# Attention with V and 64 columns of ones as weights: outputs that leave PE transposed, sums repeated 64-fold, normalisation by Exp of minus Ln

## The chip, the cores and the metric

The kernel runs on one core of one Trainium2 chip. The metric is the device time of one execution in microseconds (us); lower is better. Engines are called as the profile calls them: PE (TensorE, matmul), PEld (its weight loads, which overlap PE: 53% and 96% of the span in the kernel before), DVE (VectorE), ACT (ScalarE), POOL (GpSimd), SP (SyncE).

## The reference, cut to what matters

```python
# q, k, v: 8 batches, 8 heads, 576 tokens, 64 per head
scores = 1 / sqrt(64) * q @ k.T
mask_local   = (rel >= 0) & (rel < 32)                       # heads 0 to 3
mask_strided = (rel >= 0) & (pos % 32 equal for both tokens) # heads 4 to 7
attn = exp(scores - max); attn /= attn.sum()
x = (attn @ v) as 4608 tokens x 512
out = ((x @ w1) * (x @ w2)) @ w3 @ w_out                     # 512 -> 1024 -> 1024 -> 512
```

The masks leave little work: each query block of a local head meets one key block of 128, each group of four residue classes (72 queries) of a strided head one block of 96 keys. The products of the last two weights (w3 @ w_out) are folded into one 1024x512 weight at the start of the kernel. The large part is the feed-forward product, nine tiles of 512 tokens.

## The kernel before

Work is written as operations with an engine, an assumed duration, dependences and the buffers they take and give. A greedy scheduler inside the kernel turns them into one fixed order per engine. Each engine then runs its order, with semaphores between them. So an operation that is longer than the scheduler thought delays all that stands behind it on its engine: in the changed kernel, below, one PV starts 2.84 us after its masks are done, because other groups stand before it on PE.

The kernel divides PSUM into four single banks ("f": feed-forward groups, transposes, folding) and two double banks ("B": scores S and PV results X). A "pair" below is two heads of one batch; there are 32, 16 local and 16 strided. Each pair is computed in two halves, g = 0 and 1. The parts that the change touches, with cuts marked:

```python
plan = Plan(dict(f=NF, B=2, stg=NSTG, pte=3, asb=2, osb=3, xqs=4, w3n=4, abt=4))   # buffers of each kind
v16L = [consts.tile([P, 4, LT, D + 1], FP16, ...) for i in range(2)]    # V and one column of ones
# ...
for g in range(2):                                                      # two halves of a pair
    # S: scores, transposed (keys on partitions); one B slot
    pin(nc.tensor.matmul(sps[:, h, i * w:(i + 1) * w], kT[r_, ks:ks + P], qT[r_, hp, qs:qs + w], ...))
    # exp on ACT: PSUM -> SBUF, float16; the B slot is free again
    pin(nc.scalar.activation(out=pte[0:kr], in_=bank("B", sk)[0:kr, :, 0:288], func=AF.Exp, ...))
    # mask on DVE, float16 -> float16
    pin(nc.vector.tensor_mul(ptm..., pte..., mask...))
    # PV: the probabilities are the weights, [V|1] streams: 65 columns; queries on partitions
    pin(nc.tensor.matmul(xps[:, h, i * 65:(i + 1) * 65], ptms[pslot][0:kr, c0:c0 + P],
                         vt[0:kr, 2 * (hp % 2) + h, g * m + i, :], start=True, stop=True))
    # norm on DVE: one reciprocal per query and head, one product
    pin(nc.vector.reciprocal(out=rcp[0:w, :, 0:m], in_=xv[:, :, :, D]))
    pin(nc.vector.tensor_mul(xqs..., xv[:, :, :, 0:D], rcp...))
# U: transposes of the normalised outputs on PE, then a copy (DVE or ACT) into xT, the feed-forward input
pin(nc.tensor.transpose(ps[:, t * w:(t + 1) * w], live[("xqs", ...)]..., id16[0:w, 0:w]))
# ... feed-forward per tile of 512 tokens: 8 x (a: 4 matmuls, copy asb on ACT; b: 4 matmuls, product on DVE),
# then 4 x (o: 8 matmuls, copy osb on ACT, store issued from ACT)
```

The softmax here doesn't subtract the row's maximum and nothing guards it: scores larger than these inputs give would overflow.

## Time and profile before

| before | value | view |
|---|---|---|
| time | 283.07 us median of 2 (282.9 to 283.25) | runs |
| PE busy | 270.5 us, 96% of the span | the page, part 1 |
| ACT busy, DVE busy | 155.4 us (55%), 166.3 us (59%) | the page, part 1 |
| PE's share of the chain of waits | 83% | the page, part 4 |
| granted PE clock | full in every slice | the page, part 2 |

From the page of the kernel before: busy time per engine (us, share of the span, instructions), the granted clock in 40 slices (tenths), and the first line of the chain that ended last.

```profile
PE 270.5 (96%) x2540; PEld 150.5 (53%) x2540; DVE 166.3 (59%) x326; ACT 155.4 (55%) x291; POOL 123.2 (44%) x146
...
PEclk9999999999999999999999999999999999999999
...
PE 83%; DMA 8%; DVE 4%; SPq 1%; ACT 1%; POOL 1%; issue 0%; ACTq 0%; POOLq 0%; DVEq 0%
```

From the groups of instructions, each shape apart (line, engine, operation, out<-in, count | busy us, mean ns of one | idle before it and who ended that idle time).

```profile
L669 DVE TENSOR_TENSOR ptm<-pte,maskS 96x576 f16<-96x576 f16 x32 | 22.0, 726 | 0.2 <-ACT pte L661 0.2
L697 DVE TENSOR_TENSOR xqs<-ps_X,rcp 72x512 f16<-72x512 f32 x32 | 22.0, 687 | 1.1
L661 ACT ACTIVATE pte<-ps_S 96x576 f16<-96x576 f32 x32 | 19.1, 643 | 5.7 <-PE ps_S L650 5.7
L696 DVE RECIPROCAL rcp<-ps_X 72x8 f32<-72x8 f32 x32 | 6.4, 201 | 10.8 <-PE ps_X L682 10.5
L696 DVE RECIPROCAL rcp<-ps_X 96x6 f32<-96x6 f32 x32 | 5.9, 186 | 6.9 <-PE ps_X L682 6.5
L330 ACT ACT_TABLE_LOAD x1 | 1.3, 1283 | 0.8 <-PEq L825 0.8
```

PE is nearly always busy, and ACT and DVE wait for it. The activation tables are loaded once, in 1.28 us. What the output transposes really cost is read from the timeline, by the distance of one group's start to the next (start us, duration us, engine, line, operation); the durations themselves overlap (the first group below, 129.08 + 0.35 us, ends after the second has started at 129.26 us).

```profile
129.08 0.35 PE L682 MATMUL ps_X<-v16L,ptm 128*128 128x65 f16 x6
129.26 0.61 PE L614 MATMUL ps_T<-id,x 128*128 128x128 f16 x8
...
131.90 0.43 PE L708 MATMUL ps_U<-id,xqs 96*128 96x96 f16 x6
132.16 1.03 PE L740 MATMUL ps_a<-xT,w1h 128*128 128x512 f16 x4
```

A half of PV takes 0.18 us of PE here, and the six output transposes 0.26 us (those of a strided pair 0.27 us).

### The profile page before, as it was taken

Reading aid. Unit: us, or ns where it says so; the run is one execution under the profiler, and the core shown is the slowest. Engines: PE = TensorE matmul, PEld = TensorE weight load, DVE = VectorE, ACT = ScalarE, POOL = GpSimd, SP = SyncE. Lnnn points to the kernel's source line nnn. Section 1 sums busy time; section 2 is a strip of 40 time slices with the busy share of each in tenths; the row PEclk is TensorE's granted clock in tenths of the full one; section 3 lists DMA queues with packets and bytes.
Section 4 is the critical chain, followed back from the end, with each engine's and each line's share of the span. In section 5 each row is a group of like instructions: output and inputs, shape, how many; then the busy total and the mean of one; then the engine's idle time right before and its main releaser. Section 6 shows DMA issues by size and latency. Waiting matters only on the chain.

```text
span 282.0 us, 6430 instructions
## 1 busy us (share of the span) xinstructions
PE 270.5 (96%) x2540; PEld 150.5 (53%) x2540; DVE 166.3 (59%) x326; ACT 155.4 (55%) x291; POOL 123.2 (44%) x146
## 2 busy tenths in 40 slices
PE   4989989999999999999799999999999999999995
PEld 1468876456555555555455555555555554444443
DVE  4037486876668788856885668466746673320320
ACT  2386576448665665666357656765666543324322
POOL 5876898699669685772956352100000000000000
PEclk9999999999999999999999999999999999999999
DMA  6999999996779678978973800210021003003003
GB/s 222 323 376 358 279 357 355 240 294 235 246 185 356 170 241 243 278 248 233 337 159 102 302 2 2 94 58 0 3 112 40 0 4 147 2 0 149 0 3 149
DMA packets 53679, 48.66 MB, mean 173 GB/s; under 512 B 21008, under 2 KB 45840, under 8 KB 53648
## 3 DMA queue, kind: packets, MB, share of 16 engines
q1 hardware_dynamic: 48320, 38.81, 46.2%
q10 hardware_dynamic: 5328, 9.44, 8.9%
q8 instruction: 20, 0.33, 0.5%
q14 instruction: 11, 0.09, 0.1%
HBM read 38.80 MB, written 9.44 MB: 171 GB/s over the span
## 4 chain that ended last, share of the span: by engine, by line
PE 83%; DMA 8%; DVE 4%; SPq 1%; ACT 1%; POOL 1%; issue 0%; ACTq 0%; POOLq 0%; DVEq 0%
PE ps_a L740 22%; PE ps_b L757 21%; PE ps_o L777 21%; PE ps_X L682 5%; PE ps_T L614 4%; DMA st<-in_moe_w_dram 4%; PE ps_S L650 4%; PE ps_U L708 3%; DMA st<-in_moe_w_out_dram 3%; DVE ptm L669 3%; PE ps_mm L543 3%; DMA st<-in_k_dram 2%; SPq L293 1%; DVE xT L288 1%; DVE abt L763 0%; ACT qT L286 0%
## 5 line engine op out<-in xcount | busy, mean ns | idle before, releaser
L763 DVE TENSOR_TENSOR abt<-ps_b,asb 128x512 f16<-128x512 f32 x72 | 49.5, 688 | 53.8 <-PE ps_b L757 53.2
L740 PE MATMUL ps_a<-xT,w1h 128*128 128x512 f16 x288 | 74.0, 379 | 0.0
L757 PE MATMUL ps_b<-xT,w2h 128*128 128x512 f16 x288 | 73.9, 379 | 0.0
L286 ACT COPY asb<-ps_a 128x512 f32<-128x512 f32 x72 | 42.5, 590 | 48.0 <-PE ps_a L740 48.0
L777 PE MATMUL ps_o<-w,abt 128*128 128x512 f16 (+1 forms) x296 | 67.3, 373 | 0.0
L661 ACT ACTIVATE pte<-ps_S 96x576 f16<-96x576 f32 (+1 forms) x64 | 38.4, 648 | 12.4 <-PE ps_S L650 12.3
L757 PEld LDWEIGHTS <-w2h 128*128 128x128 f16 x288 | 27.3, 98 | 30.7
L777 PEld LDWEIGHTS <-abt 128*128 128x128 f16 x296 | 27.2, 98 | 27.0
L697 DVE TENSOR_TENSOR xqs<-ps_X,rcp 72x512 f16<-72x512 f32 (+1 forms) x64 | 39.7, 620 | 2.2
L290 POOL CAST x<-st 128x1024 f16<-128x1024 f32 x32 | 34.7, 1102 | 11.5 <-DMA st<-in_k_dram 4.1
L740 PEld LDWEIGHTS <-w1h 128*128 128x128 f16 x288 | 25.7, 98 | 23.9
L286 ACT COPY osb<-ps_o 128x512 f32<-128x512 f32 (+1 forms) x37 | 21.9, 591 | 27.3 <-PE ps_o L777 27.3
L290 POOL CAST v16L<-st 32x768 f16<-32x768 f32 (+1 forms) x32 | 27.6, 864 | 14.0 <-DMA st<-in_v_dram 4.7
L286 ACT COPY qT<-ps_T 128x512 f16<-128x512 f16 x27 | 15.8, 586 | 28.1 <-PE ps_T L614 28.0
L682 PEld LDWEIGHTS <-ptm 96*128 96x128 f16 (+1 forms) x448 | 21.4, 97 | 15.3 <-DVE ptm L669 3.5
L288 DVE COPY xT<-ps_U 128x576 f16<-128x576 f16 x30 | 17.9, 596 | 12.2 <-PE ps_U L708 12.2
L696 DVE RECIPROCAL rcp<-ps_X 72x8 f32<-72x8 f32 (+1 forms) x64 | 12.4, 193 | 17.8 <-PE ps_X L682 17.0
L290 POOL CAST v16S<-st 96x1024 f16<-96x1024 f32 x16 | 16.8, 1054 | 13.4 <-PE ps_X L682 12.4
L669 DVE TENSOR_TENSOR ptm<-pte,maskL 128x576 f16<-128x576 f16 x32 | 21.8, 713 | 0.8 <-ACT pte L661 0.7
L669 DVE TENSOR_TENSOR ptm<-pte,maskS 96x576 f16<-96x576 f16 x32 | 22.0, 726 | 0.2 <-ACT pte L661 0.2
L614 PE MATMUL ps_T<-id,x 128*128 128x128 f16 x256 | 19.1, 219 | 0.0
L543 PE MATMUL ps_mm<-woh,w3T 128*128 128x256 f16 x128 | 16.5, 273 | 0.7 <-ACT w3T L286 0.7
(65 smaller groups left out, 235.8 us busy)
## 6 DMA issues: line engine op xcount, KB each, us to landing
out_dram<-osb ACTq DMA_DIRECT2D x35, 256.0 KB, 2.0
st<-in_q_dram SPq DMA_DIRECT2D x16, 512.0 KB, 4.4
st<-in_k_dram SPq DMA_DIRECT2D x16, 512.0 KB, 7.4
st<-in_moe_w_dram SPq DMA_DIRECT2D x16, 512.0 KB, 7.9
st<-in_v_dram SPq DMA_DIRECT2D x32, 144.0 KB, 5.3
st<-in_v_dram SPq DMA_DIRECT2D x16, 256.0 KB, 5.0
st<-in_moe_w_out_dram SPq DMA_DIRECT2D x4, 512.0 KB, 7.5
st<-in_q_dram SPq DMA_DIRECT2D x8, 128.0 KB, 5.3
```

The source lines that it names most:

```text
L286: pin(nc.scalar.copy(out=out, in_=in_))
L290: pin(nc.gpsimd.tensor_copy(out=out, in_=in_))
L543: pin(nc.tensor.matmul(ps, big[f"w3T{kc // 4}"][:, kc % 4, js], big["woh"][:, kc, ns], start=(kc == 0), stop=(kc == KF - 1)))
L614: pin(nc.tensor.transpose(ps[:, c * P:(c + 1) * P], x16[(b, x, hp // 2)][:, c, h0:h0 + 2] .rearrange("p h d -> p (h d)"), id16))
L661: pin(nc.scalar.activation(out=pte[0:kr], in_=bank("B", sk)[0:kr, :, 0:288], func=AF.Exp, bias=0.0, scale=scale))
L669: pin(nc.vector.tensor_mul(ptm[0:kr, 0:576].rearrange("p (a x) -> p a x", x=w), pte[0:kr].rearrange("p h (a x) -> p (h a) x", x=w), _ap(mk ...
L682: pin(nc.tensor.matmul(xps[:, h, i * 65:(i + 1) * 65], ptms[pslot][0:kr, c0:c0 + P], vt[0:kr, 2 * (hp % 2) + h, g * m + i, :], start=True, ...
L697: pin(nc.vector.tensor_mul(xqs[0:w, 0:m].rearrange("p i h d -> p h i d"), xv[:, :, :, 0:D], _ap(rcp, 0, [[rcp.ap[0][0], w], [4, 2], [1, m] ...
L740: pin(nc.tensor.matmul(ps, w1h[:, ci, js], xT[ci][:, tok], start=(ci == 0), stop=(ci == KM - 1)))
L757: pin(nc.tensor.matmul(ps, w2h[:, ci, js], xT[ci][:, tok], start=(ci == 0), stop=(ci == KM - 1)))
L763: pin(nc.vector.tensor_mul(big[("abt", t)][:, jc, :], bank("f", f"b{t}_{jc}"), live[("asb", t, jc)]))
L777: pin(nc.tensor.matmul(ps, big[("abt", t)][:, ci, bass.ds(ts * P, P)], w34[:, ci, bass.ds(pt * nw, nw)], start=(ci == 0), stop=(ci == KF - ...
```

## The change

The intent: let [V | 64 columns of ones] be the weights and let the probabilities stream. PV then comes out with the head dimension on partitions 0 to 63, already transposed as the feed-forward part needs it, and the sum of the probabilities is repeated on partitions 64 to 127, once for each of the 64 rows. So one product per element normalises, with no transposes and no copies afterwards. The reciprocal of that 64x576 block is computed on ACT as exp(-ln(sum)). Softmax's Exp stays in PSUM in place (so the mask product now reads float32 from PSUM), both halves of S become one step that takes both B slots, and stores are issued from SyncE. The core of the diff, with cuts marked:

```diff
-    plan = Plan(dict(f=NF, B=2, stg=NSTG, pte=3, asb=2, osb=3, xqs=4, w3n=4, abt=4))
+    plan = Plan(dict(f=NF, B=2, stg=NSTG, asb=2, osb=3, rcp=2, xqs=2, w3n=4, abt=4))
-    v16L = [consts.tile([P, 4, LT, D + 1], FP16, name=f"v16L{i}") for i in range(2)]
+    v16L = [consts.tile([P, 4, LT, P], FP16, name=f"v16L{i}") for i in range(2)]
+    nc.vector.memset(v16L[0][:, :, :, D:P], 1.0)
+    nc.vector.memset(v16S[0][:, :, :, D:P], 1.0)
     ...
+            s = Sop[(b, hp)] = plan.op(f"S{nm2}", ..., take=[("B", f"S{nm2}_0"), ("B", f"S{nm2}_1")], ...)
     ...
-                    pin(nc.scalar.activation(out=pte[0:kr], in_=bank("B", sk)[0:kr, :, 0:288], func=AF.Exp, ...))
+                    pin(nc.scalar.activation(out=sps, in_=sps, func=AF.Exp, bias=0.0, scale=scale))
     ...
-                            pin(nc.tensor.matmul(xps[:, h, i * 65:(i + 1) * 65], ptms[pslot][0:kr, c0:c0 + P],
-                                                 vt[0:kr, 2 * (hp % 2) + h, g * m + i, :], start=True, stop=True))
+                            pin(nc.tensor.matmul(xps[:, h, i * w:(i + 1) * w], vt[0:kr, 2 * (hp % 2) + h, g * m + i, :],
+                                                 ptms[pslot][0:kr, h * 288 + i * w:h * 288 + (i + 1) * w],
+                                                 start=True, stop=True))
     ...
+                    xps = bank("B", pk)[D:P, :, 0:288]
+                    pin(nc.scalar.activation(out=xps, in_=xps, func=AF.Ln, bias=0.0, scale=1.0))
     ...
+                    pin(nc.scalar.activation(out=rcp, in_=bank("B", pk)[D:P, :, 0:288], func=AF.Exp, bias=0.0,
+                                             scale=-1.0))
     ...
+                    for h in range(2):
+                        o = xT[hp][hs, S * b:S * b + S]
+                        i0, i1 = xps[0:D, h, 0:288], live[("rcp", pk)][:, h]
+                        if local:
+                            o = o[:, g * 288:g * 288 + 288]
+                        else:
+                            o = o.rearrange("x (p c) -> x c p", c=n)[:, g * m:g * m + m]
+                            i0 = i0.rearrange("x (i p) -> x i p", p=w)
+                            i1 = i1.rearrange("x (i p) -> x i p", p=w)
+                        pin(nc.vector.tensor_mul(o, i0, i1))
     ...
-                plan.op(f"st{key}", {"SP": 450} if t >= cfg.get("stsp", 99) else {"ACT": 345}, fd, deps=[c],
+                plan.op(f"st{key}", cfg.get("st", {"SP": 450}), fd, deps=[c],
```

The old way through PV is kept behind a setting (`nx`: how many pairs still take it; 0 here). Staging buffers go from 9 to 7, and V of the local heads is loaded by one transfer instead of two; two bias tiles are computed in the setup that nothing reads.

## The prediction

> **What bounds it now.** TensorE. The page's first part gives PE 270.5 of 282.0 us busy (96%), DVE 166.3 (59%), ACT 155.4 (55%), POOL 123.2; the chain of waits lies 83% on PE; the granted clock is full in every slice. ACT's idle time (48.0 us before the asb copies, 28.0 before qT, 26.1 before osb) is waiting for PE and costs nothing. The groups of instructions hold one ACT_TABLE_LOAD, 1283 ns.
>
> **What the intent removes.** PE: 224 output transposes, 32 bursts of about 0.4 us less overlap, roughly 8 us; PV streams 72 or 96 columns instead of 65, giving back about 2 us. Net PE gain, an estimate: 6 us. DVE loses the reciprocals (12.4), the xqs products (39.7) and the xT copies (17.9), and gains 128 products of 64x288 (estimate 0.4 us each, 51 us); masks now read float32 PSUM, about as long as the 0.72 us they take now. The 35 stores leave ACT's queue (0.34 us issue each).
>
> **What it really adds: ACT.** Per pair of heads ACT gets two Ln and two extra Exp, 64 Ln + 64 Exp in all; the present 96x576 exp takes 643 ns, so about 0.65 us each, 83 us. Worse, they alternate with each other. The built program's order shows 129 table loads on ACT (1 before)[...]. [...] 128 x 1.283 = 164 us.
>
> ACT's sum up to the last exp(-ln), from trace durations: asb 56 x 0.59 = 33, osb 25 x 0.60 = 15, other copies 36, softmax exps 41.5, Ln and Exp 83, loads 164: about 373 us, or 11.7 us for each of the 32 pairs. All attention of a pair is one chain: S takes both PSUM slots, so the next S waits until the second norm is done: S, exp, exp, mask, PV, load, Ln, load, Exp, load, Ln, load, Exp, two products. Over 7.7 us of it is loads, Ln and Exp. PE has only some 7 us of work per pair, so ACT becomes the bound; PE idles and its 6 us gain is off the critical path.
>
> **Time.** First ACT copy at 10.8 us as now (it waits for loads); 32 x (11.7 + about 0.5 of unfilled gaps) = 390; then, after the last norm, the order leaves two tiles and a bit on PE: 212 matmuls at 0.216 us, 46 us; last eviction and store about 3 us. Sum 450 us. 80% range 425 to 495. Chances: faster 0.01, same 0.01, slower 0.98.
>
> **What would show it.** ACT busy near 395 us (about 88%) with 129 table loads of 1.28 us; PE busy share near 60%; the chain of waits mostly on ACT lines of Ln, the normalising Exp and the loads; S waiting for DVE's norm, norm waiting for ACT; PE waiting for PSUM that ACT should free. [...] The last 45 us: PE back to back, as before.
>
> **What would make it wrong.** (1) The cost of a switch. [...] in this trace the copy starts 0.02 us after the only load[...]. (2) Gaps: fixed orders of PE, DVE and ACT may interlock, 1 us more per pair is 32 us. (3) Loads that run ahead while ACT waits for PV would hide up to 1.3 us per pair: 40 us less. (4) PE's clock dropping lengthens S, PV and the tail.

Passages that no trace or run of this case shows are cut from it, with the cuts marked. None of them is a term of the sum, which stays 10.8 + 390 + 46 + 3 = 450 us; what is gone is a second possible time, for a cost of each switch beyond the load, and why the clock should fall. Some figures it uses, from the traces: four 128x512 matmuls start 0.86 us apart in the kernel before (0.216 us each); a store's issue takes 0.34 us of ACT's queue there; in the changed kernel one load stands before every Ln and one before every normalising Exp (64 and 64), and the masks take 0.75 us each. The record does not say from what the 0.4 us of the 64x288 product was estimated; the 554 ns that DVE took for 384 columns in the kernel before would make it 0.42 us. Of the risks, (3) can be seen in the changed kernel, where a load starts at 253.27 us, before PV at 254.13 us. As to (4), groups of four matmuls took 1.70 us there at a granted clock of 0.5 and 0.86 us at 1.00.

## The result, and the profile after

The changed kernel takes 499.61 us (499.48 to 499.74, 2 runs) against 283.07 us. The ratio is 1.7649, 95% interval 1.7573 to 1.7725. Ratios here and below are the mean time of one kernel's fast runs over that of the other's fast runs of the same rounds, so not quite the ratio of the quoted medians. The direction was foreseen; the time lies 50 us above the central value and just under 5 us above the range.

From the page of the changed kernel, the same three lines.

```profile
PE 345.5 (69%) x2317; PEld 176.1 (35%) x2317; DVE 263.0 (53%) x348; ACT 375.5 (75%) x491; POOL 118.2 (24%) x146
...
PEclk9977977778789577777777777777777978877999
...
ACT 35%; PE 35%; issue 19%; DVE 10%; ACTq 0%; DVEq 0%
```

From its groups of instructions.

```profile
L785 DVE TENSOR_TENSOR xT<-ps_X,rcp 64x288 f16<-64x288 f32 x128 | 120.1, 938 | 108.8 <-ACT rcp L768 108.0
L761 ACT ACT_TABLE_LOAD x64 | 82.1, 1283 | 2.6 <-DVE ptm L710 1.5
L768 ACT ACT_TABLE_LOAD x64 | 82.1, 1283 | 1.1
L761 ACT ACTIVATE ps_X<-ps_X 64x576 f32<-64x576 f32 x64 | 40.1, 627 | 4.0 <-PE ps_X L722 3.3
L768 ACT ACTIVATE rcp<-ps_X 64x576 f32<-64x576 f32 x64 | 41.4, 647 | 0.7
```

The 128 table loads inside the attention stage are there, 164 us of ACT. No engine is busy throughout any more; the chain passes through ACT, DVE and PE. ("issue" in the chain is mostly the load before the normalising Exp, which this view does not count as work: stretches of 1.26 us follow each arrival at that line.) The timeline of one strided pair's end and the next one's start shows how the steps hang together.

```profile
268.65 0.65 ACT L768 ACTIVATE rcp<-ps_X 64x576 f32<-64x576 f32 x1
269.31 1.28 ACT L761 ACT_TABLE_LOAD   x1
269.33 2.86 DVE L785 TENSOR_TENSOR xT<-ps_X,rcp 64x288 f16<-64x288 f32 x2 [1.07 <-ACT rcp L768]
270.61 0.63 ACT L761 ACTIVATE ps_X<-ps_X 64x576 f32<-64x576 f32 x1
271.25 1.28 ACT L768 ACT_TABLE_LOAD   x1
272.55 0.65 ACT L768 ACTIVATE rcp<-ps_X 64x576 f32<-64x576 f32 x1
273.23 2.86 DVE L785 TENSOR_TENSOR xT<-ps_X,rcp 64x288 f16<-64x288 f32 x2 [0.31 <-ACT rcp L768]
273.94 0.30 PE L684 MATMUL ps_S<-qT,kTS 64*128 64x72 f16 x8
276.24 0.42 PE L684 MATMUL ps_S<-qT,kTS 64*128 64x72 f16 x8 [1.99 <-DVE xT L785]
276.75 0.63 ACT L702 ACTIVATE ps_S<-ps_S 96x576 f32<-96x576 f32 x1 [1.83 <-PE ps_S L684]
```

Two things are to be seen. Load, Ln, load, Exp follow each other without a gap: each instruction starts 0.01 to 0.02 us after the one before. And the two products of a strided half take 2.86 us; those of a local half take 0.91 us, as this line from the same kernel's timeline shows.

```profile
298.42 0.91 DVE L785 TENSOR_TENSOR xT<-ps_X,rcp 64x288 f16<-64x288 f32 x2 [1.48 <-ACT rcp L768]
```

The prediction had 0.8 us for either. The first half's product lies in the shadow of the second half's loads, Ln and Exp (3.9 us); the second half's does not, and the second half of the next S waits for it. PE's part is seen a little earlier, again in the timeline of the changed kernel:

```profile
249.04 1.89 PE L847 MATMUL ps_b<-xT,w2h 128*128 128x512 f16 x4
...
249.87 1.42 DVE L710 TENSOR_TENSOR ptm<-ps_S,maskL 128x576 f16<-128x576 f32 x2 [0.46 <-ACT ps_S L702]
250.72 1.91 PE L830 MATMUL ps_a<-xT,w1h 128*128 128x512 f16 x4
...
252.43 1.92 PE L847 MATMUL ps_b<-xT,w2h 128*128 128x512 f16 x4
...
254.13 0.84 PE L722 MATMUL ps_X<-ptm,v16L 128*128 128x96 f16 x12
...
255.26 1.03 PE L830 MATMUL ps_a<-xT,w1h 128*128 128x512 f16 x4
256.12 1.03 PE L847 MATMUL ps_b<-xT,w2h 128*128 128x512 f16 x4
```

Behind S the fixed order puts feed-forward groups before PV. From start to start they take 1.70 us each at first (249.04 to 250.72, 250.72 to 252.43) and 0.86 us a little later (255.26 to 256.12): the same four matmuls take twice as long after PE's wait for S, at a granted clock that has dropped (0.5 in the trace from 247.7 to 254.4 us, 1.00 from 254.5 to 261.2 us). The softmax Exp began at 249.20 us and both masks were done by 251.29 us, but PV starts only at 254.13 us: it was PE's own order that held it. Over all 32 pairs the first PV matmul starts 69.3 us in sum after the end of the first mask, 2.2 us per pair.

Who waits for whom, in the changed kernel (total us, times, longest us):

```profile
DVE xT L785 <- ACT rcp L768: 108.0, 64, 6.6
...
PE ps_S L684 <- DVE xT L785: 68.5, 30, 3.7
```

### The profile page after: what moved, and what is told of

Its sections match the earlier page's. It is cut to its first block, busy times and chain, and to the rows that moved or that the text cites. A ratio compares the mean times of both kernels' runs of the same rounds, so it can differ in the third digit from the quotient of the medians.

```text
span 497.8 us, 6322 instructions
## 1 busy us (share of the span) xinstructions
PE 345.5 (69%) x2317; PEld 176.1 (35%) x2317; DVE 263.0 (53%) x348; ACT 375.5 (75%) x491; POOL 118.2 (24%) x146
## 4 chain that ended last, share of the span: by engine, by line
ACT 35%; PE 35%; issue 19%; DVE 10%; ACTq 0%; DVEq 0%
ACT L761 12%; PE ps_a L830 10%; PE ps_b L847 10%; DVE xT L785 8%; ACT ps_X L761 8%; ACT rcp L768 7%; PE ps_o L867 6%; ACT L768 3%; PE ps_S L684 3%; PE ps_X L722 1%; ACT asb L303 1%; PE ps_spin L326 1%; PE ps_T L641 1%; ACT kTL L303 1%; PE ps_mm L569 1%
## 5 line engine op out<-in xcount | busy, mean ns | idle before, releaser
L785 DVE TENSOR_TENSOR xT<-ps_X,rcp 64x288 f16<-64x288 f32 x128 | 120.1, 938 | 108.8 <-ACT rcp L768 108.0
L830 PE MATMUL ps_a<-xT,w1h 128*128 128x512 f16 x288 | 93.3, 456 | 12.4 <-DVE kTS L305 6.8
L847 PE MATMUL ps_b<-xT,w2h 128*128 128x512 f16 x288 | 94.2, 460 | 8.5 <-DVE kTS L305 6.3
L867 PE MATMUL ps_o<-w,abt 128*128 128x512 f16 (+1 forms) x296 | 81.4, 426 | 13.6 <-DVE kTL L305 13.6
L761 ACT ACT_TABLE_LOAD x64 | 82.1, 1283 | 2.6 <-DVE ptm L710 1.5
L768 ACT ACT_TABLE_LOAD x64 | 82.1, 1283 | 1.1
L702 ACT ACTIVATE ps_S<-ps_S 96x576 f32<-96x576 f32 (+1 forms) x64 | 39.0, 630 | 27.4 <-PE ps_S L684 26.8
L684 PE MATMUL ps_S<-qT,kTL 64*128 64x96 f16 x192 | 11.4, 236 | 60.4 <-DVE xT L785 42.2
L761 ACT ACTIVATE ps_X<-ps_X 64x576 f32<-64x576 f32 x64 | 40.1, 627 | 4.0 <-PE ps_X L722 3.3
L768 ACT ACTIVATE rcp<-ps_X 64x576 f32<-64x576 f32 x64 | 41.4, 647 | 0.7
L305 DVE COPY qT<-ps_T 128x512 f16<-128x512 f16 x30 | 20.7, 691 | 35.3 <-PE ps_T L641 35.3
L684 PE MATMUL ps_S<-qT,kTS 64*128 64x72 f16 x256 | 11.7, 224 | 30.6 <-DVE xT L785 26.3
L303 ACT COPY osb<-ps_o 128x512 f32<-128x512 f32 (+1 forms) x37 | 19.9, 579 | 13.7 <-PE ps_o L867 13.4
```

Of the source, the lines that this page charges most:

```text
L303: pin(nc.scalar.copy(out=out, in_=in_))
L702: pin(nc.scalar.activation(out=sps, in_=sps, func=AF.Exp, bias=0.0, scale=scale))
L761: pin(nc.scalar.activation(out=xps, in_=xps, func=AF.Ln, bias=0.0, scale=1.0))
L768: pin(nc.scalar.activation(out=rcp, in_=bank("B", pk)[D:P, :, 0:288], func=AF.Exp, bias=0.0, scale=-1.0))
L785: pin(nc.vector.tensor_mul(o, i0, i1))
L830: pin(nc.tensor.matmul(ps, w1h[:, ci, js], xT[ci][:, tok], start=(ci == 0), stop=(ci == KM - 1)))
```

## The experiments

The theory after reading the two traces: the time of the attention stage is that of 32 pairs, one after the other, because S needs both slots and gets the second one when the pair before is fully normalised. The links of the chain are the table loads with Ln and Exp (known), the slow product of strided pairs (mis-sized) and PE's groups between S and PV (left out). Here and in the expectations, A is the theory under test and B (or C) its rival. Rivals: one of these hides the others; the fixed orders interlock; or the chain is too long even without loads.

### Without the table switches

The edit asks at the start for one set of tables, meant to serve both Ln and Exp. With it the build places no further load: this run's trace has one, of 1.28 us, where the changed kernel has 129, and the result is correct.

```diff
+    pin(nc.scalar.preload_act_table_set("natural_log_exp_and_others"))
```

> One table load at the start of the set that serves both Ln and Exp; the order of all instructions is otherwise that of the changed kernel (1 load instead of 129). Theory A (the loads stand on the serial chain of a head pair, S, exp, mask, PV, Ln, Exp, product, S): 4 x 1.28 us leave each of 32 pairs, 164 us in all, so about 335 us (320 to 350). Rival B (the loads are hidden behind the slow products on DVE and behind PE's groups, and those carry the time): less than half comes back, above 415 us. ACT busy should fall from 375 to about 213 us in both.

Measured: correct, 364.41 us, ratio to before 1.2872. ACT busy fell from 375.5 to 209.1 us. So 135 of the 216 us are the switches. The time lies between the two ranges: it is most, as theory A has it, but 14 us above A's range, and not all of the 164 us that the loads last comes back: now something else bounds the stage. The timeline of this run shows what.

```profile
151.17 0.65 ACT L769 ACTIVATE rcp<-ps_X 64x576 f32<-64x576 f32 x1
151.72 0.64 ACT L762 ACTIVATE ps_X<-ps_X 64x576 f32<-64x576 f32 x1
151.85 2.88 DVE L786 TENSOR_TENSOR xT<-ps_X,rcp 64x288 f16<-64x288 f32 x2 [0.20 <-ACT rcp L769]
152.39 0.65 ACT L769 ACTIVATE rcp<-ps_X 64x576 f32<-64x576 f32 x1
...
155.36 2.85 DVE L786 TENSOR_TENSOR xT<-ps_X,rcp 64x288 f16<-64x288 f32 x2
```

Without loads, Ln and Exp of the second half take 1.3 us, less than the first half's products. Both products of a strided pair are now on the chain, not only the second.

### Output in runs of four

For strided heads the product writes every eighth float16 of a row, one element per 16 bytes, and takes 1.43 us for 288 elements, 5.0 ns each; for local heads it writes neighbours and takes 0.45 us, 1.6 ns each. The edit only changes the order in which the same elements are walked, so that four neighbours are written in turn:

```diff
-                            o = o.rearrange("x (p c) -> x c p", c=n)[:, g * m:g * m + m]
-                            i0 = i0.rearrange("x (i p) -> x i p", p=w)
-                            i1 = i1.rearrange("x (i p) -> x i p", p=w)
+                            o = o.rearrange("x (p c) -> x p c", c=n)[:, :, g * m:g * m + m]
+                            i0 = i0.rearrange("x (i p) -> x p i", p=w)
+                            i1 = i1.rearrange("x (i p) -> x p i", p=w)
```

> The product of the strided heads walks its output in runs of 4 adjacent float16 instead of single elements 16 bytes apart; same elements, same result, table loads left in. Theory A (the write in single steps makes the product slow: a pair of products takes 2.86 us there against 0.91 us in local heads, and the next S waits for it): the pair falls to about 1.1 us, 16 of 32 head pairs lose about 1.8 us each, the time falls by about 30 us to 468 us (455 to 480). Rival B (the slowness lies in the shift of partitions or in two operands, or is off the chain): products stay near 2.9 us or the time stays within 1% of 499.6 us.

Measured: correct, 473.04 us, ratio 1.6709; 26.6 us less than the changed kernel. From the groups of this run:

```profile
L785 DVE TENSOR_TENSOR xT<-ps_X,rcp 64x288 f16<-64x288 f32 x128 | 69.2, 540 | 133.8 <-ACT rcp L768 132.9
```

The mean fell from 938 to 540 ns; a strided pair of products takes 1.27 us in this run's timeline. It is the step of the write that was slow, not the shift of partitions or the number of operands, which stayed. (The edit also turns the order in which both operands are read, from neighbours to steps of 72 elements. That this is not the gain follows from the changed kernel: there local and strided products read in the same order and differ in the step of the write alone, 0.45 against 1.43 us.) Rival B is out. Why the step costs this much is not shown; besides neighbours and runs of four, only this one step of eight was measured.

### Both

> Both edits. Theory A (the rest of the change is sound: 6 us less PE work): PE is the bound again, 272 to 283 us, PE busy share 95% or more. Rival B (the serial chain of a head pair, which holds both slots until the second product is done, is itself too long even without loads: about 6.7 us by the sum of its links, and with PE's groups in between more): 285 to 310 us, with PE idle before S waiting for the product.

The edit is the sum of the two above. Measured: correct, 292.52 us (291.29 to 292.99, 4 runs), ratio 1.0321, interval 1.0272 to 1.0369. The two faults together are worth 207 us, more than 135 + 27: with loads in place half of the slow products is hidden, without them none is. That alone does not give the sum: 1.59 us less (2.86 to 1.27) for each of the 32 pairs of strided products is 51 us, and the edit took 72 us off (364.4 to 292.5). In the run with slow products the mean granted clock was 0.924, here 1.0, and PE's groups were shorter too (395 against 380 ns in the mean for one matmul of the first product); which part of the other 21 us that is, no run separates. What is left is a kernel 3% slower than before, so theory A was too hopeful and rival B's range holds. From its page:

```profile
PE 269.6 (93%) x2317; PEld 145.4 (50%) x2317; DVE 208.8 (72%) x348; ACT 207.4 (71%) x363; POOL 118.2 (41%) x146
```

PE is the fullest engine again, but its busy time is hardly below the 270.5 us of before, with 42.5 us more on DVE and 52 us more on ACT. The first feed-forward group starts at 50.8 us against 42.3 us. That is nearly the whole difference of the spans (291.1 and 282.0 us); from there on the two need 240.3 and 239.7 us.

### Where the last 3% are

Setup first. In this run two memsets of the ones (1.34 and 1.76 us on DVE) stand before the steps that build the mask, and matmuls without use that stand early in PE's order (the expectation below calls them warm-up) wait for these: the first useful transposes start at 13.6 us against 10.1 us. The next edit sets the mask steps ahead of the second memset and drops two bias tiles that nothing reads.

```diff
-    nc.vector.memset(v16L[0][:, :, :, D:P], 1.0)      # and the five lines after it: ones into the V tiles
+    # the same lines; those of v16S now after maskK and maskS, in a pinned order
-    for o, i in ((biasL, maskL), (biasS, maskS)):
-        nc.vector.tensor_scalar(out=o, in0=i, scalar1=-1.0, scalar2=30000.0, op0=ALU.add, op1=ALU.mult)
```

> The kernel of one table set and runs of four, with its setup put in another order: the memsets of the ones in the V tiles no longer stand on DVE before the small steps that build the mask, and two unused bias tiles are gone. Theory A (the 3.1 us of memsets delay the mask, the warm-up matmuls behind it on PE and so the first transposes, 13.6 us against 10.1 before): first transposes near 10.2 us, time down by 3 to 4 us to 288.5 to 289.5 us. Rival B (the start is bound by the loads and the casts on POOL anyway): within 1 us of 292.5 us.

Measured: correct, 291.59 us (289.41 to 292.06, 4 runs), ratio 1.0299. The transposes start at 11.1 us and the first feed-forward group at 48.3 us, 2.5 us earlier, but the kernel is only about 1 us faster in the median, and the intervals of the two ratios overlap (1.0272 to 1.0369 and 1.0251 to 1.0348): rival B's range holds, and no gain is shown. Next, the first four pairs, which must be through before any feed-forward group can start, take the old path (`nx=4`, the old results using the buffers of the new):

> As the setup run, and the first four head pairs take the old path (rows of 65, reciprocal, transposes), the other 28 the new one. Theory A (before the first feed-forward group can start, four pairs must pass one after another, and the new chain of a pair is about 1.25 us longer): first feed-forward group 5 us earlier, 283 to 285.5 us, so equal to before within 2%. Rival B (the loss at the start has another cause, loads or casts): as the setup run within 1.5 us. Neither theory expects a gain of over 1% on the kernel before: PE's occupied time after the first group is only about 2 us lower with the new path.

Measured: correct, 289.23 us (288.51 to 290.37, 4 runs), ratio 1.0222. The first feed-forward group starts at 43.4 us, as the theory said; of the 4.9 us won there only about 1.2 us arrive at the end of the span in the profiled executions (289.8 to 288.6 us), 2.4 us in the medians; that is between the ranges of A and B. The start is not all that bounds: later pairs give time back. In the timeline of this run PE is empty from 72.5 to 73.8 us and from 74.1 to 75.0 us while ACT works through an eviction, Ln, Exp, Ln, Exp in its fixed order (chain of waits of that stretch). Theory A named a real delay and overrated what it is worth.

Then the opposite cut: all 32 pairs on the old path (`nx=32`), everything else of the change kept.

> The changed kernel with all 32 head pairs on the old way through PV (rows of 65, reciprocal, transposes), the rest of the change kept: softmax Exp in place in PSUM, both halves of S as one step, stores from SyncE, slots, setup. No Ln, so one table load. Theory A (everything slow comes with the new PV and its normalisation, and the rest is neutral but for the setup, which costs up to 3 us): 281 to 287 us. Rival B (in-place Exp keeps the PSUM slot through the mask and S waits for both slots, so the rest of the change loses much by itself): over 290 us.

Measured: correct, 286.52 us (286.42 to 286.68, 4 runs), ratio 1.0127, interval 1.0080 to 1.0175. With one column of ones again, set late, and without the bias tiles:

> As the run above, with only one column of ones per head and block as before, set after the mask steps, and the unused bias tiles gone. Looks for a version that beats the kernel before. Theory A (the rest of the change is neutral): 281 to 284 us, same as before within 1%. Theory B (stores from SyncE take 35 x 0.34 us of issue from ACT and that helps): 279 us or less. Rival C (longer hold of the slots): over 286 us.

Measured: correct, 284.39 us (284.09 to 285.61, 4 runs), ratio 1.0065, interval 1.0003 to 1.0127. So the rest of the change (Exp in place, S as one step, stores from SyncE) is close to neutral in sum. What stores from SyncE bring by themselves was not tested; the gain that theory B expected of them (279 us or less) is not there. A version that beats the kernel before was not found. The new way through PV, freed of both faults, costs about 6 us against the old one in the same kernel (292.5 against 286.5 us; the runs were on different chips, and the ratios to the kernel before are 1.0321 and 1.0127). In the traces these 6 us lie before the first feed-forward group (50.8 against 45.1 us; from there on 240.3 and 239.6 us). Its gain on PE is real but small. In the run with the first four pairs on the old path, the timeline has a local half of PV at 134.86 us:

```profile
134.86 0.42 PE L720 MATMUL ps_X<-ptm,v16L 128*128 128x96 f16 x6
135.11 0.61 PE L639 MATMUL ps_T<-id,x 128*128 128x128 f16 x8
```

From start to start it takes 0.25 us, against 0.18 us before; a strided half takes 0.26 us (148.89 to 149.15 us in the same run) against 0.24 us before (143.26 to 143.50 us there). With the transposes gone a local pair saves 0.26 - 2 x 0.07 = 0.12 us of PE and a strided pair 0.27 - 2 x 0.02 = 0.23 us, 16 x 0.35 = 5.6 us in all. That is an estimate from these few groups; the medians over all groups of the two kernels differ by no more than 0.01 us from them. No run shows it as time won: PE has new gaps instead, as at 72.5 us above.

### Why not a reciprocal

One may ask why the change takes Ln and Exp at all.

```diff
-                    pin(nc.scalar.activation(out=xps, in_=xps, func=AF.Ln, bias=0.0, scale=1.0))
-                    pin(nc.scalar.activation(out=rcp, ..., func=AF.Exp, bias=0.0, scale=-1.0))
+                    pin(nc.vector.reciprocal(out=rcp, in_=bank("B", pk)[D:P, :, 0:288]))
```

> As the setup run, but DVE's reciprocal of the 64x576 sums in place of Ln and Exp on ACT (no table switch is needed). In the trace of before the reciprocals of 8 and of 6 elements per partition take 201 and 186 ns. Theory A (the difference is real: about 7.5 ns per element): 4.3 us each, 64 of them on the chain, DVE over 450 us busy, 480 to 600 us in all: this would be why the change uses Exp of minus Ln. Rival B (one pass at about 1.2 ns per element like the other float32 operations there): 0.7 us each, 280 to 292 us.

Measured (with the setup edit and runs of four): correct, 538.07 us, ratio 1.9033, in theory A's range. (Rival B's 1.2 ns per element: DVE's products in the kernel before took 726 ns for 576 elements and 687 ns for 512, which is 1.3 ns each.)

```profile
L759 DVE RECIPROCAL rcp<-ps_X 64x576 f32<-64x576 f32 x64 | 237.2, 3734 | 36.5 <-PE ps_X L719 35.9
```

3.73 us for 576 elements per partition is 6.5 ns each. The two small shapes before the change, 8 and 6 elements in 201 and 186 ns, had hinted at it: (201 - 186) / 2 = 7.5 ns for each further element. The old path needs few reciprocals, one per query and head, 8 or 6 per partition; the 64-fold sums make that 576 per partition, while Ln and Exp on ACT together take 0.63 + 0.65 = 1.28 us for the same block.

### What the prediction missed: PE's groups on the chain

To see whether PE's groups between S and PV count, this run cuts the first two feed-forward products to half their depth, which makes the result wrong (relative error 0.479).

```diff
-                for ci in range(KM):
-                    pin(nc.tensor.matmul(ps, w1h[:, ci, js], xT[ci][:, tok], start=(ci == 0), stop=(ci == KM - 1)))
+                for ci in range(2, KM):
+                    pin(nc.tensor.matmul(ps, w1h[:, ci, js], xT[ci][:, tok], start=(ci == 2), stop=(ci == KM - 1)))
```

> Wrong result on purpose: the first two products of the feed-forward part use half of the depth (2 matmuls of 4 in each group), table loads and slow products left in. The tail after the last attention step shrinks by 64 x 0.216 = 14 us in any case. Theory A (PE groups that stand between S and PV in PE's order, at 1.7 us each while the clock is low, are part of the chain): 0.9 to 1.7 us per pair more goes, so 430 to 457 us. Rival B (ACT and DVE alone make the chain; PE's groups lie in their shadow): about 484 us (478 to 490).

Measured: 462.36 us, 37.2 us less than the changed kernel, just outside theory A's range and far from B. In the traces the end of the last normalising Exp moves from 448.5 to 425.5 us, so 23 us come from the attention stage, 0.7 us per pair, and the tail after it shrinks from 49.3 to 36.3 us. PE's groups are on the chain: the wait between the end of the first mask and the first PV matmul falls from 69.3 to 35.7 us over the 32 pairs. Then the same together with runs of four:

> Wrong result on purpose: output in runs of four and half the depth in the first two feed-forward products, table loads left in. The runs of four alone gave 473.0, half depth alone 462.4 (37 less, 14 of them in the tail). Theory A (product and PE groups are separate links of one chain, so what they give adds up): 473 - 37 = 436 us (431 to 441). The prediction, which had neither link's true length, would be 450 - 14 = 436 for this kernel: the two links would then be the whole of its miss. Rival B (they hide behind each other): 450 us or more.

Measured: 439.31 us (438.59 to 440.04; wrong result), 33.7 us below the runs of four alone. The two links add up to within 3.5 us (33.7 against 37.2), and with both shortened the last normalising Exp ends at 403.9 us. The prediction had put the end of that stage at 10.8 + 390 = 401 us. That this is only some 3 us off is partly luck: the groups are halved and not gone, so 31.0 us of the wait before PV are still there, and a strided product still takes 0.64 us and not 0.4; against that, ACT is occupied for less than the prediction's sum, 354 us of the stage instead of 373. So both links are shown to be on the chain and large; that they are all that was missed is not shown.

Is it the fixed order? The scheduler was told the measured durations:

```diff
-                ln = plan.op(f"ln{nm2}_{g}", {"ACT": 650}, fl, deps=[pv], rank=1.5)
+                ln = plan.op(f"ln{nm2}_{g}", {"ACT": 1930}, fl, deps=[pv], rank=1.5)
 # likewise 1950 for the normalising Exp, and 910 or 2870 instead of 790 for the products
```

> The changed kernel, table loads and slow products left in, its scheduler told what the trace measured: 1.93 us for Ln and 1.95 for Exp with their loads (it assumed 0.65), 2.87 and 0.91 us for the two kinds of product pairs (0.79). Theory A (about 2 us per pair of ACT's idle time comes from an order made for steps that are too short): 455 to 480 us. Rival B (the serial chain of the pair sets the time in any order): 490 to 505 us.

Measured: correct, 515.31 us, ratio 1.8214. It got worse, beyond the range even of rival B. An order made with true durations does not mend it; why it is 3% worse was not followed up.

Is it the clock? The theory to be tested: if useless matmuls filled PE's wait between the halves of S, the groups behind would take 0.86 us instead of 1.70.

```diff
+                    if g == 1:
+                        for _ in range(8):
+                            pin(nc.tensor.matmul(<a shared PSUM slot>, w34[:, 0, 0:P], w34[:, 0, :], start=True, stop=True))
```

> The changed kernel, table loads and slow products left in, with 8 useless 128x512 matmuls between the two halves of S of every pair, where PE waits for the second product; all else in the same order (256 matmuls more, 55 us of PE time at full clock). Theory A (PE's idle stretch there lowers its granted clock, 0.75 in this stage, and the groups between S and PV then take 1.7 instead of 0.86 us on the chain): mean granted clock above 0.9, and although PE does more, the time falls to 455 to 480 us. Rival B (the clock is off the chain): clock up or not, 495 to 520 us.

Measured: correct, 534.00 us, ratio 1.8889, mean clock 0.855 instead of 0.80, beyond both ranges. The trace says why this did not answer the question: the filler itself waited for slots that ACT had to free (30.9 us in all before its groups, 22.0 of them for the asb copies) and took 19% of the chain. So it was tried again with a PSUM bank of its own, which leaves three shared slots; the first run is the control.

> Control: the changed kernel with three shared PSUM slots instead of four, nothing else. Both theories: somewhat slower than the changed kernel, 500 to 530 us, mean granted clock near 0.8.

> Control plus 8 useless 128x512 matmuls into a bank of their own between the two halves of S of each pair, where PE waits up to 3.7 us for the second product; they wait for nothing. Theory A (low clock stretches the groups behind S, and they are on the chain): granted clock above 0.88 in the attention stage and 10 to 40 us less than the control. Rival B (the clock does not matter to the chain): clock up, time within 5 us of the control or longer.

> Control plus 6 such matmuls before the first half of S and 8 before the second (448 in all, 97 us of PE time at full clock). Theory A: clock above 0.93 and a time below that of the run with 8 only, if PE's idle time holds them (it is about 150 us in the changed kernel). Rival B: time above the control by what does not fit into idle stretches, 0 to 30 us.

Measured, all correct: control 533.24 us (clock 0.771), 8 fillers 571.67 us (0.835), 6 + 8 fillers 615.41 us (0.846). The control is itself 33.6 us slower than the changed kernel and 3 us above its range. Theory A's times and clocks (above 0.88 and 0.93) failed. The timelines show both effects at once. The control, with b, a, b between S and PV:

```profile
280.34 1.89 PE L847 MATMUL ps_b<-xT,w2h 128*128 128x512 f16 x4
282.02 1.91 PE L830 MATMUL ps_a<-xT,w1h 128*128 128x512 f16 x4
283.73 1.22 PE L847 MATMUL ps_b<-xT,w2h 128*128 128x512 f16 x4
284.79 0.69 PE L722 MATMUL ps_X<-ptm,v16S 96*128 96x72 f16 x16
```

The run with 8 fillers, at a pair of the same kind:

```profile
302.17 3.35 PE L681 MATMUL kfill<-w 128*128 128x512 f16 x8
...
305.69 1.04 PE L850 MATMUL ps_b<-xT,w2h 128*128 128x512 f16 x4
306.57 1.03 PE L833 MATMUL ps_a<-xT,w1h 128*128 128x512 f16 x4
307.43 1.03 PE L850 MATMUL ps_b<-xT,w2h 128*128 128x512 f16 x4
308.29 0.69 PE L725 MATMUL ps_X<-ptm,v16S 96*128 96x72 f16 x16
```

The three groups take 4.45 us in the control (280.34 to 284.79) and 2.60 us behind filler (305.69 to 308.29): the slow matmuls do stretch this link, by 1.85 us there. In the control two of the groups take 1.68 and 1.71 us from start to start, the time that goes with a granted clock of 0.5 in the changed kernel; behind filler it is 0.86 to 0.88 us. But the filler took 3.3 us before the second half of S, where the control waited 1.35 us, and so put more on the chain than it won. This pair is a mild case. With three slots the order is another one, and the idle stretch that the filler was to fill has mostly gone from there: from the last matmul of the first half of S to the first of the second it is 81 us in sum over 32 pairs in the changed kernel, 26 us in the control and 97 us with 8 fillers. So the filler added 71 us in that place, and the run got 38 us longer; where the rest came back is not shown. How much of the 23 us the clock is in the changed kernel, by itself, stays open: the filler runs change the chain elsewhere, and no run here raises the clock without that.

## Why the prediction was right or wrong

- **Direction and main cause: right.** 128 further table loads of 1.283 us were predicted from the built program and one duration, and 82.1 + 82.1 us of them are in the trace. Asking for the shared set took 135 us away by itself.
- **No cost of a switch beyond its load: right.** In the changed kernel loads and activations follow each other within 0.02 us.
- **"ACT becomes the bound", 32 x (11.7 + about 0.5 of unfilled gaps): the step that failed, in its second term.** ACT was busy 375.5 us (395 predicted), only 75% of the span (88% predicted). From its first copy of qT at 13.7 us to the end of the last normalising Exp at 448.5 us it was occupied for 354.9 us, not more than the 373 us of the sum, but idle for 79.9 us: 2.5 us per pair, not 0.5. From one pair's first softmax Exp to the next one's the trace has 13.34 us in the mean ((433.73 - 20.04) / 31), not 12.2. So ACT does not set the time by being full; a chain through all three engines does, and two of its links were mis-sized.
- **"First ACT copy at 10.8 us as now": 2.9 us too early.** The changed kernel's first copy starts at 13.7 us; the longer setup (see above) was not in the prediction.
- **First mis-sized term: the product.** The estimate of 0.4 us for each 64x288 product holds for local heads (0.45 us) and fails for strided ones (1.43 us). Runs of four brought 26.6 us.
- **Second: "PE has only some 7 us of work per pair", so off the chain.** As a sum that is so, but one to three feed-forward groups stand between S and PV in PE's fixed order, often at a granted clock of 0.5 (0.80 in the mean of the whole span). Halving them brought 23 us in the stage. With both links shortened the time comes to within about 3 us of what the prediction would give for such a kernel, partly by luck, as said above. The prediction named gaps of 1 us per pair (32 us) and the falling clock among what could make it wrong; its range reached 45 us above 450, and the miss was 49.6 us.
- **Tail: right in its sum.** 46 + 3 us predicted after the last normalisation, 49.3 us measured (448.5 to 497.8 us).
- **PE's gain of 6 us off the critical path: right in size (5.6 us, an estimate from the groups read) and in that it does not show.** Even without both faults the new path is some 6 us slower than the old one.
- **Waits as listed: mostly right.** S waits for DVE's product (68.5 us), the product for ACT (108.0 us). The granted clock, named among the risks, fell to between 0.7 and 0.8 in most slices. PE's busy share is 69%, not 60%: the same matmuls at a granted clock of 0.5 are busy for longer (1.70 against 0.86 us per group of four). The chain was not mostly ACT's: 35% ACT and 19% "issue", mostly loads, against 35% PE.

## What to carry to other kernels

Before costing a new activation function, look in the built program for table loads, and ask for one set that holds all functions that alternate; here one line took 128 of 129 loads away and was worth 135 us. Where a step is serial, size every link at the step width and clock that it will really meet, the innermost step of each write first of all (here 1.43 against 0.45 us for a product, and 1.70 against 0.86 us for four matmuls), and count work on an engine that is "not the bound" if its fixed order puts it between two links. Here a saving of 5.6 us on the fullest engine came to nothing, because other engines made that engine wait; that the longer holds of the PSUM slots are the reason is argued, not shown.
